# A fused short convolution and rational mixture layer: output accumulators as two PSUM tiles, and weights rebased by a scale of 2^-112

## The chip, the cores and the metric

The kernel runs on one core of a Trainium2 chip. The metric is device time of one execution in microseconds (us). A core has five engines with a queue each: TensorE (PE, with its weight loads shown apart as PEld), VectorE (DVE), ScalarE (ACT), GpSimd (POOL) and SyncE (SP, which here only issues DMAs). Matmuls write PSUM, a small accumulator memory; DVE and ACT read it; other operands lie in SBUF.

## The reference

The input x has 8 sequences of 4096 rows and 192 columns, so 32768 rows in all. First comes a causal convolution of 7 taps over the rows, with weights from a softmax per head (8 heads of 24 columns). Its result goes through

```
h = x @ w_in                       # 192 -> 2048
P = a0 + a1*h + a2*h^2 + a3*h^3
Q = 1 + |b0|*|h| + |b1|*h^2
g = P / (Q + 1e-6)
out = g @ w_out                    # 2048 -> 192
```

`w_in` and `w_out` reach the kernel as 64-bit floats, seen as pairs of 32-bit words.

## The kernel before

The rows are cut into 64 chunks of 512. A chunk has 8 units; a unit is 256 of the 2048 hidden columns, so there are 512 units. One unit k is this work:

- `gemm1` on PE (line 512): ten matmuls into a PSUM tile `hp` of two banks (two such tiles, so unit k+2 must wait for the readers of unit k).
- On ACT five passes over 128x1024: A (line 583, |h|) and t (line 579, a square), both reading `hp`; A<-A (line 586, a square), l (line 593, Ln) and y (line 597, Exp of -l, written to PSUM). The division is thus Exp(-Ln(Q)).
- On DVE four passes, all from the helper `stt` (line 305): t<-t,cf,hp (called V in the plan), g<-t,cf,y (m), A<-A,cf,y (e) and g<-A,cf,g (g).
- `gemm2` on PE (line 521), three units later (LAG): 16 matmuls in two pairs of row blocks, the eight of pair 0 and then the eight of pair 1, which add g @ w_out into the output accumulator. Over the 8 units of a chunk the accumulator is filled.

PE's order is fixed: gemm1 of unit k, then gemm2 of unit k-3, pair 0 and pair 1. The accumulator `op` is one PSUM tile of 2 banks (line 517), pair 0 in the first bank and pair 1 in the second, in a pool with one buffer. When a chunk is full, `out_evac` (line 526) reads it twice on ACT, once for each pair (line 530, `ob`), and a DMA on SP stores each half. The first gemm2 of the next chunk writes a new `op` tile in the same place.

POOL makes the convolution of later chunks: for each tap a tensor_scalar in two halves (line 447) into a temporary, and an accumulating DMA into `acc` (line 453), six in a row for each chunk; each tap waits for the end of a given unit on DVE.

The order of ACT, DVE and POOL is written by a planner, `plan` (line 66): it simulates the engines with a table of costs and due ranks and emits instructions in the order in which it started them. The plan already takes the two pairs for separate: gemm2 of pair 0 in a new chunk depends there on the `ob` of pair 0 alone (line 154).

In the first 100 us the weights are prepared, 16 pieces, in steps between the first units (`prep`, line 380). A piece's 64-bit words are turned into 32-bit floats: a = |upper word seen as a float| (ACT), d = lower word scaled (ACT), m = maximum of a and the float with bits 0x38000000 (DVE, line 389), s = shift left by 3 and mask (DVE, line 395), o = or in the sign, and one more bit, of the upper word (DVE, line 399), r = add d (POOL), and for w_in the split in a high and a low part, h (ACT) and l (DVE).

Of the kernel before, what the change touches and what calls it, by code (L numbers as in the profile page):

```python
# [10 lines left out]
F32 = mybir.dt.float32  # L11
F32R = mybir.dt.float32r
U32 = mybir.dt.uint32
I32 = mybir.dt.int32
I64 = mybir.dt.int64
AF = mybir.ActivationFunctionType
ALU = mybir.AluOpType
# [3 lines left out]
NB, S, D = 8, 4096, 192  # L21
# [3 lines left out]
P = 128  # L25
# [10 lines left out]
NG = 6  # L36
EPS_Q = 1e-6
C_Q = 1.0 + EPS_Q
F64_MIN = float(np.uint32(0x38000000).view(np.float32))
LAG = 3  # L40
NG_BUF = LAG + 3

COST = {"c": 950, "g1": 2280, "g2": 1300, "xh": 460, "xl": 600, "S": 905, "A": 905, "B": 945, "L": 949, "Y": 950,
        "V": 1195, "m": 1196, "e": 1196, "g": 1142, "k": 3300, "kr": 400, "O": 357, "U": 1198, "Q": 2500,
        "x": 1060, "a": 900, "h": 1200, "l": 1200}
PREP = {"a": 660, "d": 660, "m": 430, "s": 420, "o": 690, "r": 1300, "h": 610, "l": 690}
PREP_ENGINE = {"a": "ACT", "d": "ACT", "m": "DVE", "s": "DVE", "o": "DVE", "r": "POOL", "h": "ACT", "l": "DVE"}
LOCKED = ("w", "g")
TAIL = {"PE": 300, "ACT": 180, "DVE": 150, "POOL": 150}
LANDING = 4800  # L50
# [7 lines left out]
NPREP = 3  # L58
# [7 lines left out]
def plan(fast):  # L66
# [3 lines left out]
    def add(name, engine, cost, deps, rank, release=0):  # L70
        locked = (engine == "POOL" and name[0] != "a") or (engine == "DVE" and name[0] in LOCKED)
        tasks[name] = (engine, cost, [d for d in deps if d], rank, release, locked)

    arrive, last = 4000, {}
    for n, (which, i) in enumerate(RAW):
        arrive += (2600 if which == "i" else 2000) + (2200 if n == 3 else 0)
        steps = "admsorhl" if which == "i" else "admsor"
        size = 1.0 if which == "i" else 0.8
        deps = {"a": [last.get(n - NPREP)], "d": [("w", which, i, "a")], "m": [("w", which, i, "a")],
                "s": [("w", which, i, "m")], "o": [("w", which, i, "s")],  # L80
                "r": [("w", which, i, "o"), ("w", which, i, "d")], "h": [("w", which, i, "r")],
                "l": [("w", which, i, "h")]}
        if n >= NRAW:
            back = ("w",) + RAW[n - NRAW]
            deps["a"] += [back + ("o",), back + ("d",)]
        for step in steps:
            add(("w", which, i, step), PREP_ENGINE[step], PREP[step] * size, deps[step], 8 * n - 60, arrive)
        last[n] = ("w", which, i, steps[-1])
# [38 lines left out]
    for k in range(NU):  # L127
        c, i = divmod(k, UPC)
# [35 lines left out]
    for name, (engine, cost, deps, rank, release, locked) in tasks.items():  # L164
        deps = [("g2", d[1], 1) if d[0] == "G" else d for d in deps]
# [9 lines left out]
    while len(order) < len(tasks):  # L175
        best = None
        for engine, names in waiting.items():
# [4 lines left out]
            t = max(clock[engine], min(ready[n] for n in names))  # L182
            name = min((n for n in names if ready[n] <= t), key=lambda n: (tasks[n][3], n))
            if tasks[name][5]:
                t = max(t, port)
            if best is None or t < best[0]:
                best = (t, engine, name)
        t, engine, name = best
# [16 lines left out]
def kernel(  # L205
# [13 lines left out]
    nc = tc.nc  # L219
# [12 lines left out]
    ps_o = ctx.enter_context(tc.tile_pool(name="ps_o", bufs=1, space=PS))  # L232
# [44 lines left out]
    def load_w(which, i):  # L277
        raw = raw_buf[RAW.index((which, i)) % NRAW].bitcast(U32)
        if which == "i":
            nc.sync.dma_start(out=raw, in_=w_in_v[:, i])  # L280
            n = W // 2
        else:
            n = 2 * D
            raw = raw[:, 0:2 * n]
            nc.sync.dma_start(out=raw.rearrange("p (f m) -> p f m", f=2), in_=w_out_v[:, i])
        raw = raw.rearrange("p (n b) -> p n b", b=2)
        pieces[which, i] = {"lo": raw[:, :, 0], "hi": raw[:, :, 1], "n": n}
# [22 lines left out]
    a = [ab_t[:, i:i + 1] for i in range(4)]  # L310
# [57 lines left out]
    wo_t = const.tile([P, FT, D], F32, name="wo_t")  # L368
# [8 lines left out]
    def body(fast):  # L377
        prepared = {key: dict(w) for key, w in pieces.items()}

        def prep(which, i, step):  # L380
            w = pieces[which, i]
            if step == "a":
                ad = apool.tile([P, 2, W // 2], I32, name="ad")
                w["a"], w["d"] = ad[:, 0, 0:w["n"]], ad[:, 1, 0:w["n"]]
                nc.scalar.activation(out=w["a"].bitcast(F32), in_=w["hi"].bitcast(F32), func=AF.Abs)  # L385
            elif step == "d":
                nc.scalar.activation(out=w["d"], in_=w["lo"], func=AF.Identity, scale=2.0 ** -29)
            elif step == "m":
                nc.vector.tensor_scalar(w["a"].bitcast(F32), w["a"].bitcast(F32), F64_MIN, None, ALU.max)
            elif step == "s":  # L390
                if which == "i":
                    w["t"] = apool.tile([P, W // 2], F32, name="tr")
                else:
                    w["t"] = wo_t[:, 2 * i:2 * i + 2].rearrange("p f m -> p (f m)")
                nc.vector.tensor_scalar(w["t"].bitcast(U32), w["a"].bitcast(U32), 3, 0x3FFFFFF8,
                                        ALU.logical_shift_left, ALU.bitwise_and)
            elif step == "o":
                t = w["t"].bitcast(U32)
                nc.vector.scalar_tensor_tensor(out=t, in0=w["hi"], scalar=0xC0000000, in1=t,  # L399
                                               op0=ALU.bitwise_and, op1=ALU.bitwise_or)  # L400
            elif step == "r":
                t = w["t"].bitcast(I32)
                nc.gpsimd.tensor_tensor(out=t, in0=t, in1=w["d"], op=ALU.add)
            elif step == "h":
                nc.scalar.copy(out=wh_t[:, i].rearrange("p a b c -> p (a b c)"), in_=w["t"])
            elif step == "l":
                nc.vector.tensor_tensor(out=wl_t[:, i].rearrange("p a b c -> p (a b c)"), in0=w["t"],  # L407
                                        in1=wh_t[:, i].rearrange("p a b c -> p (a b c)").bitcast(F32),
                                        op=ALU.subtract)
            if (step == "r" and which == "o") or step == "l":  # L410
                n = RAW.index((which, i)) + NRAW
                if n < len(RAW):
                    load_w(*RAW[n])

        CP, TMP, X, H, G, O, st, last_step = {}, {}, {}, {}, {}, {}, {}, {}
# [97 lines left out]

        def gemm2(k, pair):
            c, i = divmod(k, UPC)
            if i == 0 and pair == 0:
                O[c] = ps_o.tile([P, 4, 256], F32, name="op")
            for j in range(2):
                f = 2 * i + j
                for t in (2 * pair, 2 * pair + 1):  # L520
                    nc.tensor.matmul(O[c][:, t, 0:D], lhsT=G[k][:, j, t * P:t * P + P], rhs=wo_t[:, f, :],  # L521
                                     start=(f == 0 and t % 2 == 0), stop=(f == FT - 1 and t % 2 == 1))
            if pair == 1:
                del G[k]

        def out_evac(c, pair):
            ob = opool.tile([P, 2, D], F32, name="ob")
            o = O[c][:, 2 * pair:2 * pair + 2, 0:D]
            if fast:
                nc.scalar.activation(out=ob, in_=o, func=AF.Copy, scale=K["rO"])  # L530
            else:
                nc.scalar.copy(out=ob, in_=o)
            nc.sync.dma_start(out=out_v[c, pair], in_=ob)
            if pair == 1:
                del O[c]

        def flat(t):
            return t.rearrange("p a b -> p (a b)")
# [72 lines left out]
        with tc.manual_schedule(engines={E.PE, E.Activation, E.DVE, E.Pool}):  # L611
            for kind, *which in plan(fast):
                {"w": prep, "c": conv, "xh": conv_high, "xl": conv_low, "g1": gemm1, "g2": gemm2,
                 "O": out_evac, "x": tap, "a": tap_add, "t": tap_weights, "h": high, "l": low_part}.get(kind, partial(unit, kind))(*which)
# [65 lines left out]
```

## Time and profile before

| | us |
|---|---|
| median of 3 runs | 2666.54 (2665.88 to 2666.84) |
| profiled execution, its own time | 2666.89 |
| span of the profiled execution, first to last instruction | 2664.7 |
| PE busy | 2534.2 |
| ACT busy | 2539.2 |
| DVE busy | 2516.9 |
| POOL busy | 1235.7 |

Three engines are busy 94 to 95% of the span. Times in rows are us from the start of the span, mean durations are ns. Instructions of one engine overlap a little in the records (the next one starts before the last one's end is written), so the distance between starts says more of an engine's pace than a duration. A number in square brackets after a row is the idle time of the engine before it, with what ended it. A matmul group, as `op` x16, is one line with its first start and its whole length.

Where the units lie: the last gemm2 of a chunk and the first of the next stand side by side on PE, with one gemm1 between them. In the rows the chunk that begins with the gemm2 at 1114.96 has its gemm1 groups three units earlier, so that PE, at a chunk's boundary, computes `hp` of unit 3 of the new chunk just before gemm2 of its unit 0.

### The profile page before, as it was taken

The page shows a single profiled execution, that of the slowest core. Times are in us where ns is not written, and L with a number is a line of the kernel's source. Part 1 is how long each engine was busy: PE and PEld are TensorE (multiplying, and loading weights), DVE is VectorE, ACT ScalarE, POOL GpSimd, SP SyncE. Part 2 cuts the span into 40 slices and gives each one's busy share as a digit, 9 for nine tenths or more (in the row PEclk, how much of TensorE's full clock was granted, in tenths as well). Part 3 has the DMA queues.
Part 4 walks back from the last instruction along what each step waited for, and adds up shares of the span by engine and source line. Part 5 has one row for each costly group of instructions (what it writes and reads, how often), then busy time and mean ns, then how long its engine had stood idle before and what let it go on. Part 6 is the DMA issues. An engine that isn't in the chain of part 4 may idle for free.

```text
span 2664.7 us, 35994 instructions
## 1 busy us (share of the span) xinstructions
PE 2534.2 (95%) x13528; PEld 2299.1 (86%) x13528; DVE 2516.9 (94%) x2160; ACT 2539.2 (95%) x2739; POOL 1235.7 (46%) x1452
## 2 busy tenths in 40 slices
PE   5999999999999999999999999999999999999998
PEld 4888888888888888888888888888888888888887
DVE  8999999999999999999999999999999999999998
ACT  7999999999999999999999999999999999999997
POOL 4454454544544444545445445454454444454530
PEclk8999999999999999999999999999999999999999
DMA  5445444445444444444544544444444444444430
GB/s 156 99 98 107 101 100 99 97 104 104 92 105 101 99 103 102 98 105 93 107 96 97 107 102 99 99 97 103 104 94 104 102 98 103 102 98 104 94 76 14
DMA packets 101721, 263.96 MB, mean 99 GB/s; under 512 B 9760, under 2 KB 44832, under 8 KB 101536
## 3 DMA queue, kind: packets, MB, share of 16 engines
q0 software_dynamic: 53568, 195.06, 38.4%
q1 hardware_dynamic: 47664, 66.04, 8.5%
q8 instruction: 108, 1.77, 0.3%
q14 instruction: 77, 0.63, 0.1%
q10 hardware_dynamic: 304, 0.46, 0.1%
HBM read 41.32 MB, written 25.17 MB: 25 GB/s over the span
## 4 chain that ended last, share of the span: by engine, by line
PE 87%; ACT 8%; DVE 2%; issue 2%; DMA 0%; POOL 0%; SPq 0%; DVEq 0%; ACTq 0%
PE op L521 50%; PE hp L512 38%; ACT l L593 2%; ACT A L586 2%; ACT ob L530 2%; ACT t L579 1%; DVE g L305 1%; DVE A L305 0%; DVE t L305 0%; ACT y L597 0%; DVE wo_t L399 0%; ACT ad L385 0%; ACT A L583 0%; PE y L434 0%; DMA wb_t<-in_wband 0%
## 5 line engine op out<-in xcount | busy, mean ns | idle before, releaser
L521 PE MATMUL op<-wo_t,g 128*128 128x192 f32 x8192 | 1424.4, 327 | 100.9 <-ACT ob L530 90.3
L521 PEld LDWEIGHTS op<-wo_t,g 128*128 128x128 f32 x8192 | 1355.6, 190 | 163.8 <-ACT ob L530 116.4
L512 PE MATMUL hp<-xh,wh_t 128*128 128x512 f32 x2048 | 872.5, 426 | 15.3 <-DVE t L305 10.6
L305 DVE SCALAR_TENSOR_TENSOR g<-t,cf,y 128x1024 f32<-128x1024 f32 x512 | 655.2, 1280 | 95.6 <-ACT y L597 78.9
L305 DVE SCALAR_TENSOR_TENSOR t<-t,cf,hp 128x1024 f32<-128x1024 f32 x512 | 653.9, 1277 | 33.8 <-ACT t L579 33.8
L305 DVE SCALAR_TENSOR_TENSOR g<-A,cf,g 128x1024 f32<-128x1024 f32 x512 | 657.0, 1283 | 1.2
L305 DVE SCALAR_TENSOR_TENSOR A<-A,cf,y 128x1024 f32<-128x1024 f32 x512 | 654.0, 1277 | 0.0
L512 PE MATMUL hp<-xh,wl_t 128*128 128x512 f32 x2048 | 633.5, 391 | 0.0
L583 ACT ACTIVATE A<-hp 128x1024 f32<-128x1024 f32 x512 | 522.1, 1020 | 49.5 <-PE hp L512 33.3
L593 ACT ACTIVATE l<-A 128x1024 f32<-128x1024 f32 x512 | 542.6, 1060 | 6.2
L586 ACT ACTIVATE A<-A 128x1024 f32<-128x1024 f32 x512 | 541.6, 1058 | 0.0
L597 ACT ACTIVATE y<-l 128x1024 f32<-128x1024 f32 x512 | 525.6, 1027 | 4.2 <-DVE xl L499 0.2
L579 ACT ACTIVATE t<-hp 128x1024 f32<-128x1024 f32 x512 | 522.0, 1020 | 0.0
L447 POOL TENSOR_SCALAR tmp<-xt,wt_t,zero 128x512 f32<-128x512 f32 x496 | 377.5, 767 | 209.3 <-DVE g L305 202.6
L512 PEld LDWEIGHTS hp<-xh,wl_t 128*128 128x128 f32 x2048 | 386.1, 189 | 86.7 <-DVE wl_t L407 0.2
L512 PEld LDWEIGHTS hp<-xh,wh_t 128*128 128x128 f32 x2048 | 387.1, 189 | 80.0 <-DVE t L305 7.3
L453 POOL DMA_DIRECT2D acc<-tmp x248 | 214.9, 867 | 414.0 <-DMA acc<-xs 369.1
L512 PE MATMUL hp<-xl,wh_t 128*128 128x512 f32 x1024 | 403.4, 394 | 0.0
L447 POOL TENSOR_SCALAR xs<-xt,wt_t,zero 128x512 f32<-128x512 f32 x248 | 188.7, 767 | 205.8 <-DVE g L305 205.8
L512 PEld LDWEIGHTS hp<-xl,wh_t 128*128 128x128 f32 x1024 | 194.2, 190 | 20.4 <-DVE xl L499 0.3
L473 POOL TENSOR_SCALAR xh<-acc,one,zero 128x1024 fp32r<-128x1024 f32 x62 | 74.2, 1198 | 251.0 <-DVE g L305 245.6
L453 POOL DMA_DIRECT2D acc<-xs x124 | 109.4, 882 | 61.3 <-DMA acc<-tmp 43.1
(57 smaller groups left out, 424.3 us busy)
## 6 DMA issues: line engine op xcount, KB each, us to landing
acc<-tmp POOLq DMA_DIRECT2D x248, 512.0 KB, 4.5
acc<-xs POOLq DMA_DIRECT2D x124, 512.0 KB, 5.2
xt<-in_xt SPq DMA_DIRECT2D x62, 518.0 KB, 4.0
out<-ob SPq DMA_DIRECT2D x128, 192.0 KB, 2.6
raw<-in_w_in SPq DMA_DIRECT2D x8, 512.0 KB, 5.7
raw<-in_w_out SPq DMA_DIRECT2D x8, 384.0 KB, 4.1
xs<-in_xa ACTq DMA_DIRECT2D x1, 324.0 KB, 4.7
xs<-in_xa SPq DMA_DIRECT2D x1, 324.0 KB, 6.5
```

The costliest lines, as they stand in the source:

```text
L305: return nc.vector.scalar_tensor_tensor(out=out_, in0=a, scalar=s, in1=b, op0=op0, op1=op1)
L447: ins = nc.gpsimd.tensor_scalar(to[:, n * CH:n * CH + CH], of[:, n * XA + k:n * XA + k + CH], wt_t[:, n, k:k + 1], zero, ALU.mult, ALU.add)
L453: nc.gpsimd.dma_start(out=CP[c], in_=TMP.pop((c, k)), accum_op=ALU.add)
L473: ins = nc.gpsimd.tensor_scalar(X[c][0].rearrange("p a b -> p (a b)"), CP[c], one, zero, ALU.mult, ALU.add)
L512: nc.tensor.matmul(H[k][:, j, :], lhsT=w[:, i, part, j, :], rhs=x, start=(n == 0), stop=(n == 4))
L521: nc.tensor.matmul(O[c][:, t, 0:D], lhsT=G[k][:, j, t * P:t * P + P], rhs=wo_t[:, f, :], start=(f == 0 and t % 2 == 0), stop=(f == FT - 1 ...
L530: nc.scalar.activation(out=ob, in_=o, func=AF.Copy, scale=K["rO"])
L579: nc.scalar.activation(out=work_tile(k, "t"), in_=h, func=AF.Square, scale=K["rt"], bias=1.0)
L583: nc.scalar.activation(out=work_tile(k, "A"), in_=h, func=AF.Abs, scale=K["rA"])
L586: nc.scalar.activation(out=s["A"], in_=s["A"], func=AF.Square, bias=1.0)
L593: nc.scalar.activation(out=work_tile(k, "l"), in_=s["A"], func=AF.Ln, scale=K["rL"], bias=1.0)
L597: nc.scalar.activation(out=work_tile(k, "y"), in_=s["l"], func=AF.Exp, scale=-1.0)
```

## The change

Two edits. The accumulator becomes two tiles, `op0` and `op1`, of one bank each, one for each pair, each with its own buffer; `out_evac` takes the tile of its pair. And step m goes: ACT's absolute value multiplies by 2^-112 as well, which subtracts 0x38000000 from the word's exponent, so that s is a shift alone and o takes the sign bit only. The planner has no task m any more, and orders what is left anew.

```
-F64_MIN = float(np.uint32(0x38000000).view(np.float32))
+F64_SCALE = 2.0 ** -112
...
-PREP = {"a": 660, "d": 660, "m": 430, "s": 420, "o": 690, "r": 1300, "h": 610, "l": 690}
+PREP = {"a": 660, "d": 660, "s": 420, "o": 690, "r": 1300, "h": 610, "l": 690}
...
-                nc.scalar.activation(out=w["a"].bitcast(F32), in_=w["hi"].bitcast(F32), func=AF.Abs)
+                nc.scalar.activation(out=w["a"].bitcast(F32), in_=w["hi"].bitcast(F32), func=AF.Abs,
+                                     scale=F64_SCALE)
...
-            elif step == "m":
-                nc.vector.tensor_scalar(w["a"].bitcast(F32), w["a"].bitcast(F32), F64_MIN, None, ALU.max)
...
-                nc.vector.tensor_scalar(w["t"].bitcast(U32), w["a"].bitcast(U32), 3, 0x3FFFFFF8,
-                                        ALU.logical_shift_left, ALU.bitwise_and)
+                nc.vector.tensor_scalar(w["t"].bitcast(U32), w["a"].bitcast(U32), 3, None, ALU.logical_shift_left)
...
-                nc.vector.scalar_tensor_tensor(out=t, in0=w["hi"], scalar=0xC0000000, in1=t,
+                nc.vector.scalar_tensor_tensor(out=t, in0=w["hi"], scalar=0x80000000, in1=t,
...
-            if i == 0 and pair == 0:
-                O[c] = ps_o.tile([P, 4, 256], F32, name="op")
+            if i == 0:
+                O[c, pair] = ps_o.tile([P, 2, 256], F32, name=f"op{pair}")
...
-                    nc.tensor.matmul(O[c][:, t, 0:D], lhsT=G[k][:, j, t * P:t * P + P], rhs=wo_t[:, f, :],
+                    nc.tensor.matmul(O[c, pair][:, t % 2, 0:D], lhsT=G[k][:, j, t * P:t * P + P], rhs=wo_t[:, f, :],
...
-            o = O[c][:, 2 * pair:2 * pair + 2, 0:D]
+            o = O.pop((c, pair))[:, :, 0:D]
```

On PE, at the boundary of two chunks, the first gemm2 of the new chunk before (the numbers behind names tell buffers apart, and the waits on other engines stand in brackets):

```order
L521 MATMUL op_2347<-wo_t_184,g_2299 128x192 [waits DVE_49,PE_49,Activation_49]
L521 MATMUL op_2347<-wo_t_184,g_2299 128x192 x7
L512 MATMUL hp_2370<-xh_2083,wh_t_182 128x512 [waits DVE_49]
L512 MATMUL hp_2370<-xl_2084,wh_t_182 128x512
```

and now:

```order
L519 MATMUL op0_2338<-wo_t_184,g_2279 128x192 [waits DVE_49,Activation_49]
L519 MATMUL op0_2338<-wo_t_184,g_2279 128x192 x3
L519 MATMUL op1_2349<-wo_t_184,g_2279 128x192 [waits Activation_49]
L519 MATMUL op1_2349<-wo_t_184,g_2279 128x192 x3
L510 MATMUL hp_2361<-xh_2059,wh_t_182 128x512 [waits DVE_49]
```

The order is the same (one row here is two matmuls in the trace); one wait for ACT ahead of both pairs has become one ahead of each.

On ACT, at the boundary of chunks 7 and 8, from the A of the last gemm1 that ran ahead, before:

```order
L583 ACTIVATE A_2907<-hp_2887 128x1024 [waits PE_49]
L597 ACTIVATE y_2911<-l_2900 128x1024 [waits DVE_49,Activation_49]
L530 ACTIVATE ob_2917<-op_2646 128x384 [waits DMAHW5_49,PE_49]
L586 ACTIVATE A_2907<-A_2907 128x1024 [waits Activation_49]
L579 ACTIVATE t_2938<-hp_2887 128x1024
L593 ACTIVATE l_2941<-A_2907 128x1024 [waits Activation_49]
L530 ACTIVATE ob_2949<-op_2646 128x384 [waits DMAHW6_49]
L597 ACTIVATE y_2952<-l_2941 128x1024 [waits DVE_49,Activation_49]
```

and now:

```order
L579 ACTIVATE A_2899<-hp_2879 128x1024 [waits PE_49]
L593 ACTIVATE y_2903<-l_2892 128x1024 [waits DVE_49,Activation_49]
L528 ACTIVATE ob_2909<-op0_2637 128x384 [waits DMAHW5_49,PE_49]
L582 ACTIVATE A_2899<-A_2899 128x1024 [waits Activation_49]
L575 ACTIVATE t_2930<-hp_2879 128x1024
L589 ACTIVATE l_2933<-A_2899 128x1024 [waits Activation_49]
L528 ACTIVATE ob_2941<-op1_2648 128x384 [waits DMAHW6_49,PE_49]
L593 ACTIVATE y_2944<-l_2933 128x1024 [waits DVE_49,Activation_49]
```

Nothing moves here, nor at any later boundary; each `ob` now has a wait of its own for PE.

On DVE, in the weights' preparation, around the first V of the kernel (t<-t,cf,hp), before:

```order
L389 TENSOR_SCALAR ad<-ad 128x384
L395 TENSOR_SCALAR wo_t<-ad 128x384
L389 TENSOR_SCALAR ad<-ad 128x512
L399 SCALAR_TENSOR_TENSOR wo_t<-raw_123,wo_t 128x384
L395 TENSOR_SCALAR tr<-ad 128x512
L305 SCALAR_TENSOR_TENSOR t<-t,cf,hp 128x1024
L407 TENSOR_TENSOR wl_t<-tr,wh_t 128x512
L399 SCALAR_TENSOR_TENSOR tr<-raw_124,tr 128x512
L305 SCALAR_TENSOR_TENSOR g<-t,cf,y 128x1024
```

and now:

```order
L394 TENSOR_SCALAR wo_t<-ad 128x384
L305 SCALAR_TENSOR_TENSOR t<-t,cf,hp 128x1024
L405 TENSOR_TENSOR wl_t<-tr,wh_t 128x512
L397 SCALAR_TENSOR_TENSOR wo_t<-raw_123,wo_t 128x384
L394 TENSOR_SCALAR tr<-ad 128x512
L397 SCALAR_TENSOR_TENSOR tr<-raw_124,tr 128x512
L394 TENSOR_SCALAR wo_t<-ad 128x384
L305 SCALAR_TENSOR_TENSOR g<-t,cf,y 128x1024
```

The rows of line 389 are gone, and V stands ahead of steps of pieces that came before it. ACT's rows are shuffled in the same way in the preparation and, within a unit, up to the fifth boundary of chunks.

## Rows read from the trace of the kernel before

**Rows 1.** The page, busy time, share of the span, instructions
```profile
PE 2534.2 (95%) x13528; PEld 2299.1 (86%) x13528; DVE 2516.9 (94%) x2160; ACT 2539.2 (95%) x2739; POOL 1235.7 (46%) x1452
```

**Rows 2.** Waits, whole span: who for whom, us in total, times, longest
```profile
PE op L521 <- ACT ob L530: 90.3, 62, 2.4
```

**Rows 3.** Chunk by chunk: length, busy time (instructions) of engines, PE clock, DMA
```profile
94.67:134.44 39.77, 39.20 (x209) 35.63 (x208) 39.49 (x33) 38.20 (x42) 20.83 (x25) 1.00 0.51 104
134.44:174.34 39.90, 39.33 (x208) 35.73 (x209) 39.39 (x34) 39.02 (x43) 19.27 (x23) 1.00 0.49 102
...
256.01:298.52 42.51, 41.02 (x209) 37.43 (x209) 40.34 (x35) 38.95 (x43) 19.53 (x23) 0.96 0.47 97
298.52:339.34 40.82, 39.34 (x209) 35.74 (x209) 38.71 (x33) 39.30 (x43) 19.53 (x23) 1.00 0.48 100
...
2625.37:2664.70 39.33, 30.76 (x168) 28.22 (x168) 28.93 (x24) 25.84 (x28) 0.00 (x0) 0.98 0.06 18
```

**Rows 4.** PE around one boundary: start, length, [idle before]
```profile
1108.44 2.76 PE L521 MATMUL op<-wo_t,g 128*128 128x192 f32 x16
...
1114.96 2.87 PE L521 MATMUL op<-wo_t,g 128*128 128x192 f32 x16 [1.48 <-ACT ob L530]
...
1119.99 2.76 PE L521 MATMUL op<-wo_t,g 128*128 128x192 f32 x16
...
1139.51 2.76 PE L521 MATMUL op<-wo_t,g 128*128 128x192 f32 x16
```

**Rows 5.** ACT around that boundary and in the units behind it
```profile
1111.24 0.49 ACT L530 ACTIVATE ob<-op 128x384 f32<-128x384 f32 x1 [0.66 <-PE op L521]
...
1114.42 0.49 ACT L530 ACTIVATE ob<-op 128x384 f32<-128x384 f32 x1
...
1118.67 1.06 ACT L593 ACTIVATE l<-A 128x1024 f32<-128x1024 f32 x1
1120.18 1.02 ACT L583 ACTIVATE A<-hp 128x1024 f32<-128x1024 f32 x1 [0.46 <-PE hp L512]
...
1123.90 1.06 ACT L593 ACTIVATE l<-A 128x1024 f32<-128x1024 f32 x1
```

**Rows 6.** DVE around that boundary
```profile
1113.62 1.28 DVE L305 SCALAR_TENSOR_TENSOR t<-t,cf,hp 128x1024 f32<-128x1024 f32 x1 [0.53 <-ACT t L579]
...
1118.39 1.28 DVE L305 SCALAR_TENSOR_TENSOR t<-t,cf,hp 128x1024 f32<-128x1024 f32 x1
...
1122.16 1.28 DVE L305 SCALAR_TENSOR_TENSOR g<-t,cf,y 128x1024 f32<-128x1024 f32 x1 [1.29 <-ACT y L597]
```

**Rows 7.** Groups by line: busy, mean ns, idle before
```profile
L389 DVE TENSOR_SCALAR ad<-ad 128x512 f32<-128x512 f32 (+1 forms) x16 | 8.1, 514 | 1.8 <-ACT ad L385 1.7
```

**Rows 8.** PE in the preparation, its waits of over 1.5 us for DVE
```profile
37.69 0.80 PE L512 MATMUL hp<-xh,wh_t 128*128 128x512 f32 x1 [6.06 <-DVE t L305]
...
89.70 2.84 PE L521 MATMUL op<-wo_t,g 128*128 128x192 f32 x16 [1.66 <-DVE g L305]
```

**Rows 9.** ACT in the preparation after 18.5 us: three waits of seven
```profile
42.17 1.02 ACT L583 ACTIVATE A<-hp 128x1024 f32<-128x1024 f32 x1 [0.84 <-PE hp L512]
...
68.49 1.02 ACT L583 ACTIVATE A<-hp 128x1024 f32<-128x1024 f32 x1 [3.00 <-PE hp L512]
...
94.87 1.02 ACT L583 ACTIVATE A<-hp 128x1024 f32<-128x1024 f32 x1 [0.47 <-PE hp L512]
```

**Rows 10.** POOL, adds by DMA and what stands between chunks
```profile
1102.52 0.88 POOL L453 DMA_DIRECT2D acc<-xs  x1 [0.17 <-POOL tmp L447]
1109.57 0.86 POOL L453 DMA_DIRECT2D acc<-tmp  x1 [6.17 <-DMA acc<-xs]
...
1116.26 1.20 POOL L473 TENSOR_SCALAR xh<-acc,one,zero 128x1024 fp32r<-128x1024 f32 x1 [4.15 <-DVE g L305]
...
1119.25 0.87 POOL L453 DMA_DIRECT2D acc<-tmp  x1 [0.30 <-POOL tmp L447]
1124.35 0.88 POOL L453 DMA_DIRECT2D acc<-xs  x1 [0.60 <-DMA acc<-tmp]
```

More of the change, by code (lines that the diff above doesn't have):

```diff
@@ L45 @@
         "x": 1060, "a": 900, "h": 1200, "l": 1200}
-PREP = {"a": 660, "d": 660, "m": 430, "s": 420, "o": 690, "r": 1300, "h": 610, "l": 690}
-PREP_ENGINE = {"a": "ACT", "d": "ACT", "m": "DVE", "s": "DVE", "o": "DVE", "r": "POOL", "h": "ACT", "l": "DVE"}
+PREP = {"a": 660, "d": 660, "s": 420, "o": 690, "r": 1300, "h": 610, "l": 690}
+PREP_ENGINE = {"a": "ACT", "d": "ACT", "s": "DVE", "o": "DVE", "r": "POOL", "h": "ACT", "l": "DVE"}
 LOCKED = ("w", "g")
@@ L76, in plan @@
         arrive += (2600 if which == "i" else 2000) + (2200 if n == 3 else 0)
-        steps = "admsorhl" if which == "i" else "admsor"
+        steps = "adsorhl" if which == "i" else "adsor"
         size = 1.0 if which == "i" else 0.8
-        deps = {"a": [last.get(n - NPREP)], "d": [("w", which, i, "a")], "m": [("w", which, i, "a")],
-                "s": [("w", which, i, "m")], "o": [("w", which, i, "s")],
+        deps = {"a": [last.get(n - NPREP)], "d": [("w", which, i, "a")], "s": [("w", which, i, "a")],
+                "o": [("w", which, i, "s")],
                 "r": [("w", which, i, "o"), ("w", which, i, "d")], "h": [("w", which, i, "r")],
@@ L533, in out_evac @@
             nc.sync.dma_start(out=out_v[c, pair], in_=ob)
-            if pair == 1:
-                del O[c]
         def flat(t):
```

## The prediction

> **What bounds the kernel now.** The page first: PE, ACT and DVE are all busy 94 to 95% of the span [rows 1], so the shares alone name no bound; the stage has to be looked at. The table chunk by chunk shows one stage repeated: a chunk lasts 40.82 us, from 298.52 on also in the mean of 57 ((2625.37 - 298.52) / 57) [rows 3]. In it the starts of PE's gemm2 groups tell the pace: from 1119.99 to 1139.51 there are four units, 4.88 us each, with no idle time of PE in front of any [rows 4]. Eight such units would be 39.04 us. The rest, 40.82 - 39.04 = 1.78 us, lies at one place: from 1108.44, the last gemm2 of a chunk, to 1114.96, the first of the next, are 6.52 us instead of 4.88, and to the following one 5.03 [rows 4]. PE sits idle for 1.48 us of it, and what ends the idle time is ACT's `ob`; the list of waits has this 62 times, 90.3 us in all [rows 2]. So PE is the bound inside a chunk, and at the boundary the accumulator is.
>
> Why it waits: `ob` of pair 0 starts at 1111.24, after ACT has sat idle 0.66 us until PE had done both pairs (1108.44 + 2.76 = 1111.20). `ob` of pair 1 starts three passes later, at 1114.42, and lasts until 1114.91 [rows 4, 5]. PE's next gemm2, though only pair 0 of it comes first, starts 0.05 us after that, since both pairs stand in one tile.
>
> **The accumulator, step by step.** With two tiles, `ob` of pair 0 needs the first eight of the 16 matmuls, done by about 1108.44 + 1.38 = 1109.82, before ACT comes to it. Its idle 0.66 us goes, and everything up to the next cross wait moves up by it: `ob` of pair 0 to 1110.58 (done 1111.07), of pair 1 to 1113.76 (done 1114.25). PE is free at 1114.96 - 1.48 = 1113.48. Pair 0 is then long released, and starts at once; pair 1 follows 1.38 us later, at 1114.86, 0.6 us after its own `ob`. So the wait goes whole, and the group is followed at 4.88 us by the next.
>
> What is late next? ACT: its A of the next `hp` can start 1.78 us sooner by PE, at 1118.40, but ACT reaches it only a pass after its l (1118.67 - 0.66 = 1118.01), at 1118.95, so it lags PE by 0.55 us. From A at 1120.18 to l at 1123.90 are four passes in 3.72 us, 0.93 each, five in 4.65 against PE's 4.88 [rows 5]; it makes up 0.23 a unit, and has caught up in three units out of eight. DVE: V at 1113.62 waited 0.53 us for ACT's t; that t comes 0.66 earlier, so V starts at about 1113.0. From 1113.62 to 1118.39, V to V, DVE runs four passes in 4.77 us without a pause [rows 6]; eight units take 38.16 of 39.04, 0.88 to spare. The 1.29 us that it waits for y at 1122.16 shrinks to about 0.7: y is one ACT pass behind the late A, so ends near 1120.9, where DVE is free near 1120.15. That is inside the 0.88. PE's next gemm1 but one needs that V's end, about 1114.3, and starts at 1115.8: 1.5 us of slack. I take 39.04 us a chunk, with nothing left of the wait. For a pause that I have overlooked the bounds are 0 and 0.86 us a chunk: 39.90 us is what the chunk from 134.44 took, where `ob` of pair 1 stood nearer to that of pair 0 and both were still waited for [rows 3].
>
> From the start of the second chunk's gemm2 (94.67) to that of the last chunk (2625.37) are 62 chunks and 2530.7 us [rows 3]; at 39.04 they are 2420.5, a gain of 110.2. It includes the one chunk at 42.51, where the granted PE clock was 0.96 in the mean and not 1.00 [rows 3]. The last chunk's 39.33 us stay: its end is DVE's, which there stands as far behind PE as before.
>
> The Trainium skill (Perfetto Trace Analysis, section Identifying the Most-Contended Engine) takes the engine with the highest occupancy for the bound, and for TensorE takes the busy share of weight loads in place of matmuls. By it ACT would bind the steady chunk (39.30 us of 40.82, against 35.74 for the loads), and a chunk would not get below 39.30: 62 x 0.26 = 16 us less gain, 2569.6. The rows speak against taking 39.30 for work: the same passes, 42 of them, are busy for 38.20 us in the chunk from 94.67 [rows 3], since a record that starts behind its own input is longer; I keep 39.04, and this as a rival.
>
> **The maximum and the mask.** Sixteen m passes go from DVE, 8.1 us busy [rows 7]. The multiplication rides in ACT's pass, and the other two passes keep their number and shape; for these I take no change, since no operand is added that is read from memory; at worst each of the 32 costs or saves as much as a tenth of a pass, 0.05 us, or 1.6 us in all. In the first 95 us PE waits for DVE up to 6.06 us at a time, last by 1.66 at 89.70 [rows 8], so there is something to win; but ACT, which loses no pass, runs almost without a break from 18.5 us on. It waits seven times from there to 94.87; the two longest are 0.84 and 3.00 us, and the last, 0.47, is the longest of the other five [rows 9], so no more than about 6 us can be gained. The new order of the preparation could also lose: V now stands ahead of weight steps of earlier pieces, and a weight that comes late stops a gemm1 or gemm2. I bound it by one wait as long as ACT's longest, 3 us lost, and take 3 us gained, half of what ACT's waits allow. The second chunk's gemm2 then starts at 91.7.
>
> **Sum.** 91.7 + 2420.5 + 39.3 = 2551.5 us of span. Around the span lie 2666.89 - 2664.7 = 2.2, so 2553.7 for an execution like the profiled one, which stood 0.35 above the median of the runs: 2553.4, say 2553.5 us, 4.2% less than before.
>
> **The rivals.**
> - ACT or DVE sets the pace. ACT has to put two `ob` into each chunk, 0.76 us of starts, and its slack is some 1 us a chunk; DVE's is 0.88, of which the replay uses 0.7. For it: both are that near. Against it: in the replay both are back in step before the next boundary. If a chunk takes 39.30, the time is 2569.6; if 39.4, 2576.
> - Pair 1 still waits. The slack of 0.6 us is that of one boundary; if `ob` of pair 1 comes one ACT pass later (0.93), 0.33 us of wait stays per boundary, 20 us, 2574; at the bound of 0.86 it is 53 us, 2607. Against it: nothing in ACT's order at the steady boundaries has moved.
> - The change doesn't do what it says: the wait for both `ob` stays, because pair 0's release is signalled late or a later wait takes its place 1.48 us on. Then only the preparation is left: 2660 to 2667. Against it: the new PE rows have a wait for ACT ahead of each tile.
> - Slower: the chain of POOL's adds. The six accumulating DMAs of a chunk follow each other's landing; most gaps are about 5.1 us (1119.25 to 1124.35), but one is 7.05 (1102.52 to 1109.57), with POOL waiting 6.17 for the landing. From the sixth add to the first of the next chunk at least a landing (5.1) and what lies between the starts of xh and that add (1116.26 to 1119.25, 3.0) pass, 8.1 us [rows 10]. Now the chain takes 4 x 5.1 + 7.05 + 8.1 = 35.6 us at least, 3.4 below the new chunk. If the denser cadence stretched every gap to 7.05, a chunk would take 5 x 7.05 + 8.1 = 43.4, 2.5 us over 40.82, and the time would be 2664 + 62 x 2.5 = 2820. It decides from a mean gap of 6.2 us, and costs time from 6.55. Against it: the DMA share of 0.48 would rise only with the pace, to 0.50, and the chunk at 94.67 had 0.51 without harm [rows 3].
>
> The Trainium skill (TensorE: Matmul & The Clock Gate, section A second HAM failure mode: psum-queue depth-cycling) says that short repeated idle times between matmul groups can make PE's clock go back and forth, so that filling them would give more than the idle time. By that rule the steady chunks would have lost clock too; they stand at 1.00 with their 1.48 us pause [rows 3], so I add nothing.
>
> **How the numbers follow.** Forecast, 39.04 us a chunk: 0.72, with 2547 to 2561 (3 us more or 6 us less gain in the preparation, the small passes, 0.05 us a chunk). ACT or DVE sets the pace, up to 2576: 0.13. Pair 1 still waits, up to 2607: 0.08. No effect: 0.04. Slower: 0.03. A range of 2546 to 2576 holds the forecast and most of the first rival, about 0.85. A measurement of this kernel tells 0.2%, 5 us, from no change: faster 0.94, the same 0.03 (the no-effect case without its best part), slower 0.03.
>
> **What would show it.** Right: gemm2 groups of PE 4.88 us apart across boundaries, no row of PE waiting for `ob`, ACT's 0.66 us in front of the first `ob` gone, the chunk 39.0 us, PE busy over 98%. In the preparation: the second chunk's first gemm2 between 88 and 98 us. Wrong: PE idle before `hp` with DVE's t as the releaser (DVE is the bound), PE idle between pair 0 and pair 1 (the second `ob`), ACT without any wait for `hp` in a whole chunk (ACT is the bound), or POOL's xh waiting for a DMA at each chunk and PE for POOL.

## The result, and the profile after

The changed kernel takes 2553.55 us, the median of four runs (2552.47 to 2554.43), against 2666.61 (2665.88 to 2666.84) for the kernel before on the same chip. The ratio is 0.9576, with a 95% interval of 0.956 to 0.9593: 4.2% faster. 2553.5 was forecast. The forecast was a sum of three stretches; beside each stands what the profiled execution (2553.43 us, span 2551.3) shows:

| stretch, us | before | forecast | after |
|---|---|---|---|
| start to the second chunk's first gemm2 | 94.67 | 91.7 | 91.61 |
| 62 chunks, second to last-but-one | 2530.7 | 2420.5 | 2420.95 |
| last chunk | 39.33 | 39.3 | 38.74 |
| span | 2664.7 | 2551.5 | 2551.3 |

The page's busy line after, which answers to [rows 1]. Lines of the program moved a little: gemm1 is now L510, gemm2 L519, `ob` L528, the DVE helper still L305.

```profile
PE 2514.7 (99%) x13528; PEld 2302.7 (90%) x13528; DVE 2491.4 (98%) x2144; ACT 2512.0 (98%) x2739; POOL 1243.0 (49%) x1452
```

PE went from 95 to 99% with the same 13528 matmuls. The list of waits after, all rows for PE (total us, times, longest):

```profile
PE op L519 <- DVE g L305: 9.3, 3, 6.6
PE y L432 <- DVE cf L300: 8.0, 1, 8.0
PE hp L510 <- DVE t L305: 7.6, 4, 6.0
PE hp L510 <- ACT wh_t L403: 3.1, 1, 3.1
PE hp L510 <- ACT ad L385: 2.4, 1, 2.4
PE hp L510 <- DVE wl_t L405: 0.7, 1, 0.7
```

No row names `ob`, where 90.3 us in 62 waits stood before [rows 2]; what is left is in the first 100 us and the last chunk.

Table by chunk after: length; busy us of PE, PEld, DVE, ACT, POOL; PE clock, DMA share, GB/s (the columns of [rows 3]). The first row is the second chunk, the second a steady one, the third the last.

```profile
91.61:130.65 39.04, 39.04 (x209) 35.82 (x208) 38.76 (x33) 38.82 (x42) 19.43 (x24) 1.00 0.45 94
1107.07:1146.11 39.04, 39.04 (x209) 35.81 (x208) 38.35 (x33) 38.85 (x43) 19.65 (x23) 1.00 0.51 107
2512.56:2551.30 38.74, 30.61 (x169) 28.12 (x167) 29.76 (x25) 26.52 (x30) 0.00 (x0) 1.00 0.06 18
```

A chunk is 39.04 us, PE is busy for all of it, and its clock is at 1.00 (2.4 GHz) in every steady chunk. PE's gemm2 around the boundary that [rows 4] show, the first of the new chunk at 1107.07:

```profile
1102.19 2.76 PE L519 MATMUL op<-wo_t,g 128*128 128x192 f32 x16
1107.07 2.76 PE L519 MATMUL op<-wo_t,g 128*128 128x192 f32 x16
1111.95 2.76 PE L519 MATMUL op<-wo_t,g 128*128 128x192 f32 x16
```

The boundary is 4.88 us like every other unit, where it was 6.52. ACT in the two units around it (the answer to [rows 5]):

```profile
1104.26 0.48 ACT L528 ACTIVATE ob<-op 128x384 f32<-128x384 f32 x1
...
1107.42 0.50 ACT L528 ACTIVATE ob<-op 128x384 f32<-128x384 f32 x1
1107.79 1.05 ACT L593 ACTIVATE y<-l 128x1024 f32<-128x1024 f32 x1
1108.74 1.04 ACT L579 ACTIVATE A<-hp 128x1024 f32<-128x1024 f32 x1
1109.64 1.07 ACT L575 ACTIVATE t<-hp 128x1024 f32<-128x1024 f32 x1
1110.55 1.10 ACT L582 ACTIVATE A<-A 128x1024 f32<-128x1024 f32 x1
1111.69 1.06 ACT L589 ACTIVATE l<-A 128x1024 f32<-128x1024 f32 x1
```

No idle time stands in front of the first `ob`. The second ends at 1107.92. The eight matmuls of pair 1 in the new chunk start 1.30 us after 1107.07:

```profile
1108.37 1.46 PE L519 MATMUL op<-wo_t,g 128*128 128x192 f32 x8
```

That is 0.45 us to spare. (Half of the group's recorded length, 1.38 us, would give 0.53; but its matmuls start 0.16 us apart, and the length includes the last one's own 0.33.) It is worth looking at the last two rows too: `l` starts 1.14 us after the pass whose result it reads, while passes that read something older start 0.90 to 0.95 apart. This becomes the point below on which the prediction was off.

### The profile page after: what moved, and what is told of

It is laid out like the page before. It is cut to its first block, busy times and chain, and to the rows that moved or that the text cites. A ratio compares the mean times of both kernels' runs of the same rounds, so it can differ in the third digit from the quotient of the medians.

```text
span 2551.3 us, 36055 instructions
## 1 busy us (share of the span) xinstructions
PE 2514.7 (99%) x13528; PEld 2302.7 (90%) x13528; DVE 2491.4 (98%) x2144; ACT 2512.0 (98%) x2739; POOL 1243.0 (49%) x1452
## 4 chain that ended last, share of the span: by engine, by line
PE 96%; ACT 2%; DVE 1%; issue 1%; DMA 0%; SPq 0%; DVEq 0%; ACTq 0%
PE op L519 51%; PE hp L510 45%; DVE g L305 0%; DVE A L305 0%; ACT A L582 0%; ACT A L579 0%; DVE t L305 0%; ACT y L593 0%; ACT ad L385 0%; ACT l L589 0%; ACT t L575 0%; ACT ad L388 0%; PE y L432 0%; DMA wb_t<-in_wband 0%; ACT wh_t L403 0%
## 5 line engine op out<-in xcount | busy, mean ns | idle before, releaser
L519 PE MATMUL op<-wo_t,g 128*128 128x192 f32 x8192 | 1415.9, 326 | 9.3 <-DVE g L305 9.3
L519 PEld LDWEIGHTS op<-wo_t,g 128*128 128x128 f32 x8192 | 1358.5, 190 | 50.2 <-issue 7.0
L510 PE MATMUL hp<-xh,wh_t 128*128 128x512 f32 x2048 | 872.1, 426 | 13.1 <-DVE t L305 7.6
L305 DVE SCALAR_TENSOR_TENSOR g<-t,cf,y 128x1024 f32<-128x1024 f32 x512 | 654.5, 1278 | 40.7 <-ACT y L593 35.9
L305 DVE SCALAR_TENSOR_TENSOR g<-A,cf,g 128x1024 f32<-128x1024 f32 x512 | 657.6, 1284 | 0.9
L305 DVE SCALAR_TENSOR_TENSOR t<-t,cf,hp 128x1024 f32<-128x1024 f32 x512 | 653.9, 1277 | 0.9 <-ACT t L575 0.9
L305 DVE SCALAR_TENSOR_TENSOR A<-A,cf,y 128x1024 f32<-128x1024 f32 x512 | 653.9, 1277 | 0.0
L510 PE MATMUL hp<-xh,wl_t 128*128 128x512 f32 x2048 | 633.0, 390 | 0.7 <-DVE wl_t L405 0.7
L445 POOL TENSOR_SCALAR tmp<-xt,wt_t,zero 128x512 f32<-128x512 f32 x496 | 383.5, 788 | 184.6 <-DVE g L305 177.5
L510 PEld LDWEIGHTS hp<-xh,wl_t 128*128 128x128 f32 x2048 | 386.3, 189 | 87.0 <-DVE wl_t L405 1.1
L510 PEld LDWEIGHTS hp<-xh,wh_t 128*128 128x128 f32 x2048 | 387.4, 189 | 77.2 <-ACT ad L388 6.4
L510 PE MATMUL hp<-xl,wh_t 128*128 128x512 f32 x1024 | 403.0, 394 | 0.0
L510 PEld LDWEIGHTS hp<-xl,wh_t 128*128 128x128 f32 x1024 | 194.3, 190 | 20.3
```

The lines of the kernel that those rows point to most:

```text
L305: return nc.vector.scalar_tensor_tensor(out=out_, in0=a, scalar=s, in1=b, op0=op0, op1=op1)
L445: ins = nc.gpsimd.tensor_scalar(to[:, n * CH:n * CH + CH], of[:, n * XA + k:n * XA + k + CH], wt_t[:, n, k:k + 1], zero, ALU.mult, ALU.add)
L510: nc.tensor.matmul(H[k][:, j, :], lhsT=w[:, i, part, j, :], rhs=x, start=(n == 0), stop=(n == 4))
L519: nc.tensor.matmul(O[c, pair][:, t % 2, 0:D], lhsT=G[k][:, j, t * P:t * P + P], rhs=wo_t[:, f, :], start=(f == 0 and t % 2 == 0), stop=(f ...
```

## The experiments

They ask four things: which edit brought what (the first two), whether the second `ob` was the wait (the next two), what is the bound now and by how much (three that add work and one that takes some away), and what the start hangs on.

**e1_split_only.** The kernel before with the two tiles; maximum and mask kept.

```
-            if i == 0 and pair == 0:
-                O[c] = ps_o.tile([P, 4, 256], F32, name="op")
+            if i == 0:
+                O[c, pair] = ps_o.tile([P, 2, 256], F32, name=f"op{pair}")
```

> The kernel before with the two accumulator tiles alone; the weights keep maximum and mask. Theory (the gain is the sum of two independent terms, 110.2 us from PE's wait for ob and 3 us from the preparation): 2553.5 + 3 = 2556.5 us, between 2554 and 2559; steady chunk 39.04 us, no row of PE waiting for ob. Rival (the new order from the preparation also helped the boundaries): over 2570, steady chunk above 39.3.

Measured 2556.67 us (2555.97 to 2557.51), ratio 0.959 [0.9574, 0.9606]: 109.8 us below the 2666.42 of the kernel before, measured beside it, against the 110.2 of the forecast. The waits for `ob` are gone.

**e2_scale_only.** The changed kernel with one accumulator tile again; the scale kept.

```
-            if i == 0:
-                O[c, pair] = ps_o.tile([P, 2, 256], F32, name=f"op{pair}")
+            if i == 0 and pair == 0:
+                O[c] = ps_o.tile([P, 4, 256], F32, name="op")
```

> The changed kernel with one accumulator tile for both pairs again; only the maximum and the mask are gone. Theory: 2666.6 - 3.1 = 2663.5 us, between 2661 and 2666; the first gemm2 of the second chunk at about 91.6 us, steady chunk still 40.82 us with PE's 1.48 us wait for ob. Rival (the two edits need each other, the order of the preparation being worth something only without the boundary waits): 2666 to 2668.

Measured 2663.52 us (2662.97 to 2665.71), ratio 0.9992 [0.9982, 1.0002]. The median is 2.9 us lower, but by its interval this run alone does not tell the gain from none. Its waits have the old row back:

```profile
PE op L519 <- ACT ob L528: 91.9, 63, 2.4
```

The other way to see the scale is to take e1 against the changed kernel, which differ by it alone: their runs do not overlap, and the medians are 3.1 us apart, where those of the kernel before, measured beside each, differ by 0.2. In the traces the second chunk's first gemm2 starts at 94.43 in e1 and 91.61 after, 2.8 us apart. In e2 it starts at 92.92 and not at the 91.6 expected, 1.75 earlier than before; PE there already waits 0.57 us for `ob`. Another 1.7 us by which e2's trace is shorter are the chunk of 42.51 us [rows 3], which takes 40.81 here at a granted clock of 1.00. The medians add up, 109.8 + 2.9 = 112.7 of the 113.1 measured for both; that the scale is worth as much with one tile as with two is not shown.

**e3_second_late.** The changed kernel; ACT's second `ob` placed behind `l` of the next unit.

```
-            add(("O", c, pair), "ACT", COST["O"], [("g2", c * UPC + UPC - 1, pair)],
-                8 * ((c + 1) * UPC) + (19 if pair else -30))
+            add(("O", c, pair), "ACT", COST["O"], [("g2", c * UPC + UPC - 1, pair)]
+                + ([("L", c * UPC + UPC + 2)] if pair and c < NCH - 1 else []),
+                8 * ((c + 1) * UPC) + (20.5 if pair else -30))
```

> The changed kernel with the second ob two ACT passes later at every boundary (behind A and y of the units that follow). In the changed kernel it ends 0.53 us before PE's pair 1 starts. Theory (PE has no slack, so a wait counts whole): it ends 1.85 us later, 1.3 us too late, so PE waits 1.3 us between pair 0 and pair 1 at each of 63 boundaries: 2553.5 + 63 x 1.35 = 2639 us, between 2620 and 2650. Rival (ACT sets the pace as much as PE, a wait of PE is partly free): under 2600.

Measured 2639.67 us (2638.87 to 2640.43), ratio 0.9899 [0.9883, 0.9916]. PE's gemm2 at a boundary and the next one, here L520; the x16 group falls into its two pairs:

```profile
1103.34 1.46 PE L520 MATMUL op<-wo_t,g 128*128 128x192 f32 x8
1105.94 1.57 PE L520 MATMUL op<-wo_t,g 128*128 128x192 f32 x8 [1.14 <-ACT ob L529]
...
1146.41 1.57 PE L520 MATMUL op<-wo_t,g 128*128 128x192 f32 x8 [1.14 <-ACT ob L529]
```

Pair 0 starts at once and pair 1 waits: a chunk is 1146.41 - 1105.94 = 40.47 us, 1.43 more, near the 1.35 expected. So with two tiles each pair waits for its own `ob` only, and the second one still costs time when it comes later than the 0.45 us that it has to spare.

**e4_order_only.** The kernel before, one tile; the second `ob` moved up to one pass behind the first.

```
-                8 * ((c + 1) * UPC) + (19 if pair else -30))
+                8 * ((c + 1) * UPC) + (-29 if pair else -30))
```

> The kernel before, one accumulator tile, maximum and mask kept; only the second ob gets the due rank next to the first, so that ACT runs it one pass behind the first and not three. Theory (what PE waited for was the end of the second ob; the tile only decides which of the two): it ends at about 1113.1 on the old time scale, before PE is free at 1113.5, so PE's wait goes without any second tile; ACT keeps its 0.66 us of waiting for both pairs in each chunk, which its slack has to carry: 2556 to 2575 us. Rival (the tile is what counts, an order can't stand in for it): over 2600.

Measured 2573.39 us (2572.09 to 2575.52), ratio 0.965 [0.9634, 0.9666]. With a second `ob` that comes early, one tile costs no wait for `ob` either; so what PE waited for was the end of the later `ob`. The order alone brings 93.0 us of e1's 109.8: inside the range expected, near its top. Most of what is left is a new wait. ACT's t ends at 1118.24, but the planner now lets DVE's g run ahead of V (first fence, DVE), and the next gemm1 starts when V ends at 1120.34 (second fence, PE):

```profile
1116.55 1.28 DVE L305 SCALAR_TENSOR_TENSOR A<-A,cf,y 128x1024 f32<-128x1024 f32 x1
1117.86 1.28 DVE L305 SCALAR_TENSOR_TENSOR g<-A,cf,g 128x1024 f32<-128x1024 f32 x1
1119.06 1.28 DVE L305 SCALAR_TENSOR_TENSOR t<-t,cf,hp 128x1024 f32<-128x1024 f32 x1
```

```profile
1117.59 2.76 PE L521 MATMUL op<-wo_t,g 128*128 128x192 f32 x16
1120.39 0.50 PE L512 MATMUL hp<-xh,wh_t 128*128 128x512 f32 x1
...
1122.79 2.76 PE L521 MATMUL op<-wo_t,g 128*128 128x192 f32 x16
```

This unit takes 5.20 us instead of 4.88, 0.32 more; at the next boundary it is 0.07 more (1156.95 to 1161.90). Over 62 chunks the mean is 39.29 us, 0.24 above e1's, and the rest of the difference between the two traces stands at the start and in the last chunk. That V's place is the cause is read from these rows and was not tried.

**e5_act_one_more** and **e6_act_three_more.** The changed kernel with one, or three (`range(3)`), unused copies of 128x384 on ACT behind each second `ob`.

```
+            if pair == 1:
+                for n in range(1):
+                    nc.scalar.copy(out=junk[:, n], in_=ob)
```

> The changed kernel with one more ACT pass in each chunk, a copy of 128x384 from the second ob tile, right behind it; it is not part of the result. By the starts of ob it costs ACT about 0.4 us a chunk. Theory (PE sets the pace and ACT has a little to spare, about 0.5 us a chunk): 2553 to 2558 us, PE groups still 4.88 us apart across boundaries. Rival (ACT sets the pace as well, since in the changed kernel no row of it waits for hp any more): the whole 0.4 us a chunk, 63 x 0.4 = 25 us, 2579 us.

> The same with three such copies in each chunk into one tile, about 1.4 us of ACT. Theory (ACT has some 0.5 us a chunk to spare, the rest counts): 0.9 us a chunk, 2553.5 + 57 = 2610 us, between 2595 and 2625. Rival (ACT sets the pace): 2640 us. Rival (ACT has 1.84 us a chunk, eight times the 0.23 us that a unit gave back): 2553.5 us.

Measured 2573.6 us (2572.33 to 2573.64), ratio 0.9654 [0.9638, 0.967], and 2641.94 us (2641.44 to 2643.12), ratio 0.9911 [0.9895, 0.9928]. Both lie above their theory's range, which gave ACT 0.5 us to spare. In both ACT sets the pace, and has no idle time in a steady chunk; e6 came out near its rival's 2640, e5 below its rival's 2579. ACT in e5 at a boundary:

```profile
1114.63 0.50 ACT L529 ACTIVATE ob<-op 128x384 f32<-128x384 f32 x1
1115.16 0.51 ACT L535 COPY junk<-ob 128x384 f32<-128x384 f32 x1
1115.58 1.02 ACT L597 ACTIVATE y<-l 128x1024 f32<-128x1024 f32 x1
```

From the second `ob` to `y` are 0.95 us here, and in e6 2.03 (1102.41 to 1104.44), against 0.37 after (1107.42 to 1107.79): 0.58 and 1.66 us more a chunk. In time they cost 20.1 and 88.4 us, 0.32 and 1.40 in each of 63 chunks. Both leave the same remainder, 0.26 us: that is the slack that ACT had. In e5 the price is paid where the second `ob` comes too late for pair 1, and PE shows it as a longer group:

```profile
1113.68 3.06 PE L520 MATMUL op<-wo_t,g 128*128 128x192 f32 x16
...
1153.04 3.06 PE L520 MATMUL op<-wo_t,g 128*128 128x192 f32 x16
```

1153.04 - 1113.68 = 39.36 us a chunk, 0.32 over 39.04. In e6 three units are longer (5.35, 4.93 and 5.75 us from the group at 1101.32 on), and in the third PE waits 0.57 us for V.

**e7_dve_one_more.** The changed kernel with an unused add of 128x512 on DVE once a chunk, 0.60 us.

```
+                if k % UPC == 3:
+                    nc.vector.tensor_tensor(out=junk, in0=s["A"][:, 0:CH], in1=s["A"][:, CH:], op=ALU.add)
```

> The changed kernel with one more DVE pass in each chunk, an add of 128x512 in SBUF behind g of the chunk's fourth unit, about 0.6 us; it is not part of the result. Theory (DVE has 0.88 us a chunk and its 0.61 us wait for y lies ahead of the added pass, so it runs up to 0.3 us a chunk short, unless the wait shrinks when DVE is late): 2553 to 2573 us. Rival (DVE sets the pace): 63 x 0.6 = 38 us, 2591 us.

Measured 2575.53 us (2574.79 to 2575.97), ratio 0.966 [0.9644, 0.9677], 2.5 us over the top of what the theory of DVE's slack allowed and far below the rival. The reason is ACT again. Its row of waits, and one of them:

```profile
ACT y L594 <- DVE A L306: 35.9, 63, 0.8
```

```profile
1137.15 1.03 ACT L594 ACTIVATE y<-l 128x1024 f32<-128x1024 f32 x1 [0.58 <-DVE A L306]
```

`y` has one PSUM tile, so ACT can write the next `y` only when DVE's e has read the last. ACT stands for 0.58 us; less its slack of 0.26 are 0.32 a chunk, 20 us, and 22 were measured. That DVE's delay passes through ACT is the trace's; that DVE alone would have had room is not shown.

**e8_second_conv_later.** The changed kernel with the second chunk's convolution on PE one unit later.

```
-SECOND, SECOND_LAG = 2, 3
+SECOND, SECOND_LAG = 3, 3
```

> A try at a faster version: the changed kernel with the second chunk's convolution one unit later (SECOND 3 instead of 2), since what PE still waits for lies in the preparation (6.56 us for g of the third unit, 6.0 us for a t), where that convolution's result holds y of the third unit back. Theory (y of the third unit comes sooner and the wait shrinks by 2 to 5 us): 2548 to 2552 us. Rival (the work in the preparation fills ACT anyway and the wait moves to the next unit): 2552 to 2555 us.

Measured 2553.03 us (2552.72 to 2553.32), ratio 0.9576 [0.956, 0.9592]: no difference from the changed kernel, as the rival had it. PE's longest waits for DVE's t and g are 7.6 and 7.1 us, where those after are 6.0 and 6.6:

```profile
PE op L519 <- DVE g L305: 9.0, 2, 7.1
PE hp L510 <- DVE t L305: 7.6, 1, 7.6
```

The waits have other places and lengths and nearly the same sum, 16.6 us against 16.9.

**e9_nine_matmuls.** The changed kernel with nine of the ten gemm1 matmuls of a unit.

```
-                for n, (w, part, x) in enumerate(terms):
+                some = terms[0:5 - j]
+                for n, (w, part, x) in enumerate(some):
```

> The changed kernel with nine matmuls in gemm1 of a unit and not ten; left out is the last correction term of the second half, so the result is a little less exact. PE has 0.228 us less to do in a unit, 1.83 us in a chunk. Theory (PE sets the pace in the changed kernel, but ACT follows it with only 0.26 us a chunk to spare, as both runs with added ACT passes gave): the chunk falls to 38.78 us and no further, 2553.5 - 63 x 0.26 = 2537 us, between 2530 and 2545; ACT without a pause, PE with small waits. Rival (PE alone sets the pace, ACT's lack of slack is a matter of where the passes were added): 2553.5 - 115 = 2438 us. Rival (ACT or DVE set the pace already): 2553 us.

Measured 2539.15 us (2538.55 to 2540.45), ratio 0.952 [0.9504, 0.9536]. PE has some 0.23 us less to do in each of 512 units, 1.8 a chunk; the time falls by 14.4 us, 0.23 a chunk. ACT in it, from `ob` to `ob` a chunk later:

```profile
1098.88 0.48 ACT L530 ACTIVATE ob<-op 128x384 f32<-128x384 f32 x1
...
1120.26 1.09 ACT L591 ACTIVATE l<-A 128x1024 f32<-128x1024 f32 x1
1121.38 1.03 ACT L595 ACTIVATE y<-l 128x1024 f32<-128x1024 f32 x1
...
1137.67 0.48 ACT L530 ACTIVATE ob<-op 128x384 f32<-128x384 f32 x1
```

and PE at the same boundary:

```profile
1100.18 1.46 PE L521 MATMUL op<-wo_t,g 128*128 128x192 f32 x8
1102.60 1.57 PE L521 MATMUL op<-wo_t,g 128*128 128x192 f32 x8 [0.95 <-ACT ob L530]
```

The chunk is 38.79 us, no row of ACT in it has idle time in front, and PE waits for `ob` once more. So ACT's own pace is 38.79 us, 0.25 below the 39.04 that PE sets in the changed kernel: another reading of the slack, from the other side.

## Why the prediction was right, and where it was not

**The wait.** Shown. It was the second `ob` on which PE sat, by way of one tile (e3, e4), and with two tiles pair 0 passes and pair 1 comes in time, 0.45 us to spare for 0.6 forecast. (The forecast had its start 0.08 us late, at half of the recorded length.) The term was 110.2 us; e1 measured 109.8. What the 62 chunks after have over 62 x 39.04, 0.47 us, is nearly all at one boundary, where pair 1 did wait, PE's group is longer and the chunk takes 39.46:

```profile
208.73 3.03 PE L519 MATMUL op<-wo_t,g 128*128 128x192 f32 x16
```

DVE's wait for `y` behind the boundary, 1.29 us in [rows 6], was forecast at 0.7 and is 0.61:

```profile
1114.61 1.28 DVE L305 SCALAR_TENSOR_TENSOR g<-t,cf,y 128x1024 f32<-128x1024 f32 x1 [0.61 <-ACT y L593]
```

**The step that failed is ACT's slack.** The prediction had ACT behind PE by 0.55 us after a boundary, making up 0.23 us a unit and in step after three units; its rival gave ACT a slack of some 1 us a chunk. The first three units came out so. Their `A<-hp` start at 1112.65, 1117.30 and 1121.95, 4.65 us apart against PE's 4.88:

```profile
1112.65 1.00 ACT L579 ACTIVATE A<-hp 128x1024 f32<-128x1024 f32 x1
...
1117.30 1.02 ACT L579 ACTIVATE A<-hp 128x1024 f32<-128x1024 f32 x1
```

But that pace does not hold for the chunk. ACT waits for `hp` only in the last units before the next boundary, and the first short stop is here, five units on:

```profile
1130.63 1.06 ACT L589 ACTIVATE l<-A 128x1024 f32<-128x1024 f32 x1
1131.67 1.02 ACT L579 ACTIVATE A<-hp 128x1024 f32<-128x1024 f32 x1
```

1.04 us apart where the same two are 0.94 to 0.96 apart in the units before. One more follows before the boundary, 1.09 us apart at 1141.43; both together are some 0.2 us, all that ACT stands still for PE in this chunk. The error is in the 0.93 us a pass. That was a mean over passes none of which reads the pass just ahead of it. In the ACT rows of e9's chunk five of 40 do, and start 1.08 to 1.13 us behind it, 5.51 us together. The chunk then adds up: 35 others at 0.93 are 32.55, the two `ob` 0.37 each, 0.74, and the sum is 38.80, where 38.79 were measured. At 0.93 for all 40 it would be 37.94, and the slack 1.10. So the slack is 0.26 and not some 1; a unit with such a pair makes up 0.06 and not 0.23. The time came out right since 0.26 is still above nothing: the margin was a quarter of what the prediction thought it had, and that it was enough was luck.

The trace of the kernel before had such a pair, just ahead of the passes that the prediction counted. The `l` of [rows 5] at 1118.67 reads the pass in this row, and starts 1.12 us behind it:

```profile
1117.55 1.09 ACT L586 ACTIVATE A<-A 128x1024 f32<-128x1024 f32 x1
```

The prediction set the rival of 39.30 us aside because a record that starts behind its own input would be longer. The rows do not say that: the lengths of the 42 ACT records add up to 42.5 us in the chunk from 94.67 and 42.4 in the one from 298.52. What differs is that the first has no pass right behind the one that it reads, and the second has five, which start later.

The Trainium skill (ScalarE: Activation LUTs, section What ACT_TABLE_LOAD costs) gives 93 ns by which back-to-back ACTIVATEs overlap. For passes on older data the trace agrees (records of 1.05, starts 0.95 apart); for a pass that reads the one just ahead it does not, with 1.08 to 1.14 us between starts.

**The rivals.** That ACT or DVE sets the pace did not come about, but came within 0.26 us a chunk of it; e5, e6 and e9 show ACT in that place as soon as PE has less to do or ACT more. By occupancy ACT, at 38.85 us of 39.04 against 35.81 for weight loads, would bind the steady chunk, as the Trainium skill has it (Perfetto Trace Analysis, section Identifying the Most-Contended Engine). The time of e9 says that PE bound it down to 38.79, and ACT from there on. That pair 1 still waits shows clearly at one boundary of 63. That the change has no effect is out. For POOL's chain, the slower case, here are its adds through one chunk and the step behind them:

```profile
1112.40 0.88 POOL L451 DMA_DIRECT2D acc<-tmp  x1 [0.30 <-POOL tmp L445]
...
1142.11 0.86 POOL L451 DMA_DIRECT2D acc<-tmp  x1 [4.93 <-DMA acc<-xs]
1148.43 1.20 POOL L471 TENSOR_SCALAR xh<-acc,one,zero 128x1024 fp32r<-128x1024 f32 x1 [3.48 <-DVE g L305]
```

Five gaps in 29.71 us are 5.94 each, against the 6.2 from which it would have decided; some of them are waits for DVE and not for a landing. `xh` is released by DVE here and in most chunks, by a landing in 6 of 62, and PE has no wait for POOL. The chain has room, though less than the prediction's 4 x 5.1 + 7.05 = 27.5 us suggest: before, the five gaps up to the add at 1109.57 [rows 10] took 31.1 us, and only two of them were near 5.1.

**The preparation.** 3 us were taken between bounds of -3 and 6; 3.1 were measured between e1 and the changed kernel, and 2.9 by e2, whose interval does not tell them from none. In e1, which keeps the maximum, PE's waits are

```profile
PE op L521 <- DVE g L305: 11.1, 4, 6.7
PE hp L512 <- DVE t L305: 10.4, 2, 6.0
PE y L434 <- DVE cf L302: 7.7, 1, 7.7
PE hp L512 <- ACT wh_t L405: 4.7, 2, 3.1
```

33.9 us, and 31.1 after: 2.8 less, by which the second chunk also starts sooner. The first two rows lose 4.6, among it the wait ahead of gemm2 at 89.70 [rows 8]; the others give 1.8 back. That half of ACT's waits was the right share was an estimate that happened to fit: no run shows a reason for a half. The last chunk is 0.6 us shorter than taken, for which no cause was sought; in the traces of the experiments it lasts from 38.7 to 42.5 us.

## What to carry to other kernels

When an accumulator's halves are drained and refilled one after the other, give each half a tile of its own: what is waited for is the tile's last reader, not the half's. Moving the late reader forward does most of the same, but may push another instruction into the path, as in e4. Before trusting a slack on an engine, add up its chunk from starts with the dependent pairs apart from the others, and test it by adding a known bit of work: two sizes that leave the same remainder give the slack.

## What the runs showed of the hardware

- A pass on ACT over 128x1024 that waits for no other engine starts 0.90 to 0.97 us after the one before it, but 1.08 to 1.14 if it reads that one's result. DVE shows the same: in e4's rows g, which reads the A written just before (1116.55), starts 1.31 us later, and the V behind it 1.20.
- The one chunk that took 42.51 us at a mean granted clock of 0.96 before [rows 3] has no counterpart after: the 62 chunks lie within 0.5 us of 62 x 39.04 in all. Its first group, at 256.01, stands behind PE's longest wait for `ob`, 2.43 us, and takes 4.55 us where the group of [rows 4] takes 2.87. The wait alone does not explain it: in e2 PE waited 2.4 us for `ob` too, and the granted clock stayed at 1.00. Why it fell in the kernel before is open.
